# Linear-attention recurrence into a dropless MoE: the first six steps of the recurrence issued from a written-out table instead of the loop

## The chip, the core and the metric

The kernel runs on one core of a Trainium2 chip. The core has five engines that each work through a queue of their own, in order: PE (matrix multiply), DVE (VectorE, elementwise work, scans and reductions), ACT (ScalarE, exponentials, logarithms and copies), POOL (GpSimd, small elementwise work and indirect DMAs) and SP (SyncE, which issues nearly all the loads). An instruction starts when the one before it on its engine is done and the semaphores it waits for are there. So the order in which the program hands pieces of work to an engine decides what waits behind what.

The metric is the device time of one execution in microseconds (us), the median over several runs. An execution takes a little longer than the span between its first and its last profiled instruction.

## What is computed

The input is `q`, `k`, `v`, `f_logit` of shape (4, 8, 768, 48): batch, heads, tokens, channels. The reference runs a gated recurrence over the tokens, and sends its output through a mixture of eight experts in which every token goes to one expert:

```python
f = 1.0 / (1.0 + np.exp(-f_logit))
for t in range(S):                                   # S = 768
    state = f[:, :, t, :, None] * state + einsum('bhd,bhe->bhde', k[:, :, t], v[:, :, t])
    y[:, :, t] = einsum('bhd,bhde->bhe', q[:, :, t], state)
x = y.transpose(0, 2, 1, 3).reshape(3072, 384)
logits = x @ w_gate                                  # (3072, 8)
expert_idx = argmax(logits)
gate_w = softmax(logits)[expert_idx]
out = gate_w * (relu(x @ w1[expert_idx]) @ w2[expert_idx])   # w1: 384x1024, w2: 1024x384
```

## The kernel before, in words

**Tiling.** The 768 tokens are cut into 6 chunks of 128. A *unit* is one chunk of two of the four batches; there are NU = 12 units, and units 0, 2, 4, ... and 1, 3, 5, ... are two independent chains of states. A unit's `q`, `k` and `f` tile is 128 partitions by 8 segments by 128 tokens. Inside a chunk the recurrence becomes matrix work: with the running sum of the logarithms of `1 + exp(-f)` along the tokens, `k` is multiplied by the exponential of the sum ("r", growth) and `q` by the exponential of minus the sum ("dec", decay), and then a masked product of `k` and `q` gives the weights within the chunk.

**The pieces of one unit**, with the function, its line in the profile, its engine and its tile:

- `steps` L476 and `log` L484: ACT, exponential and logarithm of `f` into `g`
- `total` L491: DVE, the scan along the tokens, `g` to `sum`; it reads two tensors in SBUF (`g` and `cap`)
- `growth` L505: ACT, `r`, a tile with one buffer; `decay` L520: ACT, written over `g`
- `by_r` L509: `k <- k * r`, on POOL (on DVE for unit 0); it reads two tensors in SBUF
- `by_decay` L532: `q <- q * dec`, on DVE; it reads two tensors in SBUF
- `ends` L515 and `last_decay` L527: POOL, copies of 128x8
- `score` L543: PE, `s`, 16 products of `k` and `q`, in two halves a = 0, 1
- `mask` L549: DVE, four copies under a mask from PSUM into `at`; one input lies in SBUF
- `keys` L558: PE, transposes of `k`; `keep` L563: ACT, copies of them into `kn`
- `within` L571: PE, `yt` from `at` and `v`, in two halves; `before` L592: PE, the part of `yt` from the old state
- `added` L608: PE, `dp` from `kn` and `v`; `update` L623/L625: DVE, the new `state`, and then L627: POOL, `state` times `last`
- `settle` L633: ACT, `yt` to `ys`; `rows` L663: PE, transposed rows and gate logits `xp`, with a small DVE reduction L671 each half; `lay` L693/L688: ACT, rows into `xr`
- for every second unit the routing: `choose` (DVE, six small instructions, L214 to L222), `weigh` (ACT), `count` (PE, L226/L227), `place` and `fill` (DVE, nine small instructions, L233 to L260), `send` (POOL, indirect DMAs into `xs`).

`warm` L708 puts products of a zero tile on PE that nobody uses.

**What sets the order.** The block stands under `manual_schedule` for all five engines: each engine runs its instructions in the order in which the Python code calls them. Before the change the prologue issues units 0 to 2 piecewise by hand. Then one loop, `for n in range(1, NU + 2)`, issues for every step the scores, keys and masks of unit n, the halves of `within` of unit n - 1, the rows of unit n - 2, `by_r`, `ends`, `decay`, `last_decay` and `by_decay` of unit n + 1, `total` and `growth` of unit n + 2, `steps` of unit n + 3 and the loads of units n + 2 to n + 5. A dozen `if n == 1`, `if n == 2` and `1 < n < 4` in it shift pieces in the first steps.

One detail of `by_r` matters for the change. If the list `routed` holds an instruction, `by_r` takes it out and makes its POOL instruction wait for it:

```python
        def by_r(u, part=whole, on=nc.gpsimd):
            k = units[u]["k"][:, part]
            ins = on.tensor_tensor(k, k, units[u]["r"][:, part], op=OP.mult).ins
            if routed:
                tc.add_manual_dep(ins, routed.pop().name, SYNC, reason="the port of both")
```

The loop appends to `routed` the last instruction of `choose` (L222) or of `fill` (L260), from step 3 on. On DVE these stand shortly before the masks of the step. After the recurrence (units done at about 128 us) come the eight experts, PE work with the weights w1 and w2 streamed in.

Of the kernel before, what the change touches and what calls it, by code (L numbers as in the profile page):

```python
# [1 line left out]

# [8 lines left out]
F32 = mybir.dt.float32  # L11
# [3 lines left out]
OP = mybir.AluOpType  # L15
# [110 lines left out]
def kernel(  # L126
# [280 lines left out]
    def load_pads(e):  # L407
# [10 lines left out]
        tc.declare_no_dep(ins, group="xs", reason="no row is written twice")  # L418
        tc.add_to_no_dep_group("xs", ins)

    with ExitStack() as st:
        ld = st.enter_context(tc.tile_pool(name="ld", bufs=1))
        wk = st.enter_context(tc.tile_pool(name="wk", bufs=2))
# [99 lines left out]

        def last_decay(u):
            x = units[u]
            x["last"] = wk.tile([128, SEG], F32, name="last", bufs=3)
            nc.gpsimd.tensor_copy(x["last"], x["dec"][:, :, C - 1])  # L527

        def by_decay(u, part=whole):
# [35 lines left out]
        def within(u, a):  # L565

            x = units[u]
            if a == 0:
                x["yt"] = yt
            for p, h, _ in heads():  # L570
                nc.tensor.matmul(  # L571
                    x["yt"][DP * (h ^ a) : DP * (h ^ a) + D, a, p],
                    lhsT=x["v"][:, a, 2 * p + h],
                    rhs=x["at"][:, a, h, p],
                    start=p == 0,
                    stop=x["old"] is None,
                    skip_group_check=True,
                )
# [38 lines left out]
        def update(u):  # L617

            x = units[u]
            new = wk.tile([128, SEG, D], F32, name="state", bufs=4)  # L620
            last = _bc(x["last"], 2, D)
            if x["old"] is None:
                nc.vector.tensor_copy(new, x["dp"])  # L623
            else:
                nc.vector.tensor_tensor(new, x["dp"], x["old"], op=OP.add)  # L625
            states[u % 2] = new
            return lambda: nc.gpsimd.tensor_tensor(new, new, last, op=OP.mult)  # L627

        def settle(u):
            x = units[u]  # L630
# [64 lines left out]
        st.enter_context(tc.manual_schedule(engines=ordered))  # L695

        nc.scalar.preload_act_table_set("natural_log_exp_and_others")
        load(0, "f", ab)
        load(0, "kq")
        load(1, "f")  # L700
        load_first_consts()
        load(1, "kq")
        for i in (1, 0):
            nc.gpsimd.memset(scores[i], 0.0)
        def warm(count):

            for _ in range(count):
                nc.tensor.matmul(yt[:, 0, 0], lhsT=pad[:, 0:C], rhs=pad[:, 0:C], start=True, stop=True)  # L708

        warm(24)  # L710
        for part in ab:
            steps(0, part)
            total(0, part)
        load(2, "f")
        load(0, "v")
        for part in ab:
            growth(0, part)
            by_r(0, part, nc.vector)
            decay(0, part)
            by_decay(0, part)  # L720
        ends(0)
        last_decay(0)
        for part in ab:
            steps(1, part)
        load(3, "f")
        load(2, "k")
        load(1, "v")
        load(2, "q")
        load(3, "q")

        def early_banks():

# [38 lines left out]
            del sends[: len(now)]  # L771


        score(0, 0)
        score(0, 1)
        keys(0)
        warm(12)
        for part in ab:
            total(1, part)
        for a in range(2):  # L780
            for h in range(2):
                mask(0, a, h)
        for part in ab:
            growth(1, part)
            by_r(1, part)
        for part in ab:
            decay(1, part)
            by_decay(1, part)
        ends(1)
        last_decay(1)  # L790
        steps(2)
        total(2)
        keep(0)
        steps(3, logs=False)
        growth(2)
        load_consts()
        load(3, "k")
        load(4, "f")
        load(2, "v")
        load(5, "f")  # L800
        load_gate()

        for n in range(1, NU + 2):
            here, back, last = n, n - 1, n - 2
            ahead = n + 1 < NU
            state = n < NU - 2
            rt = None
            if here < NU:
                units[here]["old"] = states[here % 2]
            if 2 <= last:  # L810
                settle(last)
            if later and later[0] < NU - 1:
                later[1].weigh()
            if here < NU:
                for a in range(2):
                    score(here, a)
            if ahead and n != 2:
                by_r(n + 1)
                ends(n + 1)
            if decayed:  # L820
                decayed()
                decayed = None
            if sends:
                scatter_some(n)
            if n == NU - 2:
                soon = [load_rows(first[e]) for e in range(EARLY)]
            if n == 1:
                units[0]["old"] = None
                added(0)
                update(0)()  # L830
            if ahead and not 1 < n < 4:
                decay(n + 1)
                last_decay(n + 1)
            if state:
                keys(here)
                keep(here)
            if n == 2:
                growth(n + 1)
                by_r(n + 1)
                ends(n + 1)  # L840
            if 1 < n < 4:
                decay(n + 1)
                last_decay(n + 1)
            if here < NU:
                for a in range(2):
                    for h in range(2):
                        mask(here, a, h)
            if n == 1:
                log(3)
                within(0, 0)  # L850
                within(0, 1)
                settle(0)
            if n + 3 < NU:
                steps(n + 3)
            if later and n >= NU - 1:
                settled(*later)
                later = None
                scatter_some(NU)
            if 2 < n < NU - 2:
                total(n + 2)  # L860
            if n == NU - 2:
                by_decay(n + 1)
            first_half = 1 < n < NU - 2
            if first_half:
                within(back, 0)
            if 0 <= last:
                rt = rows(last, later[1] if later else None)
                lay(last)
            if later and n == NU - 2:
                settled(*later)  # L870
                later = None
                scatter_some(NU)
            if ahead and n < NU - 2:
                by_decay(n + 1)
            if n == 2:
                total(n + 2)
            if rt:
                rt.choose()
                if n < NU - 2:
                    routed.append(rt.latest)  # L880
                if n >= NU - 1:
                    rt.weigh()
            if later:
                settled(*later)
                routed.append(later[1].latest)
                later = None
            for a in range(int(first_half), 2):
                if 0 < back < NU:
                    within(back, a)
            if n == 2:  # L890
                settle(1)
            if n + 2 < NU and n != 1:
                growth(n + 2)
            if n == NU + 1:
                widen(soon[0], weights[0], early_h, range(3, 7))
            if n == NU:
                turn_early(soon[0])
            if state:
                added(here)
                decayed = update(here)  # L900
            if n == 1:
                total(3)
            if back < NU:
                before(back)
            if rt:
                later = (n, rt)
                if n >= NU - 1:
                    rt.count(turns("rp", [128, 2, rt.n, E]))
                if n >= NU:
                    settled(*later)  # L910
                    later = None
            if n == NU:
                early_h = early_banks()
                widen(soon[0], weights[0], early_h, range(3))
            if n == NU + 1:
                widen(soon[0], weights[0], early_h, range(7, NF))
                turn(soon[1])
            if n == 1:
                load(n + 3, "q")
            if n + 3 < NU:  # L920
                load(n + 3, "k")
            if n + 2 < NU:
                load(n + 2, "v")
            if 1 < n and n + 3 < NU:
                load(n + 3, "q")
            if n + 5 < NU:
                load(n + 5, "f")
            if n == 1:
                load_first_pads()
            if n in (8, 10):  # L930
                load_first_weights((n - 8) // 2)
                load_second_weights((n - 8) // 2)
# [395 lines left out]
```

## Time and profile before

| | |
|---|---|
| median of 9 runs | 401.79 us (400.85 to 403.5) |
| the profiled execution | 401.01 us, of which the span is 399.2 us |
| granted TensorE clock over the span | 0.986 |
| busy over the span: PE / DVE / ACT / POOL | 382.9 / 169.5 / 103.2 / 116.7 us |
| the chain that ended last | PE 87%, DMA 5%, DVE 2%, issue 2%, all else 1% or less each |
| where the chain first stays on PE for long | from 41.90 us (`dp`, L608) |

A row of the timeline reads: start in us, duration in us, engine, line, operation, output and input tiles, shapes, count, and in brackets the idle time of the engine just before it with what ended that idle time. A row of the stages reads: from:to, length, then for PE, PEld (weight loads), DVE, ACT and POOL the busy us and the instruction count, then the granted PE clock, the DMA share and GB/s.

### The profile page before, as it was taken

To read this page: it belongs to the slowest core of one execution; us is meant where nothing else is said; L and a number is where in the kernel's file an instruction comes from. 1 tells how busy PE (TensorE), PEld (TensorE's weight loads), DVE (VectorE), ACT (ScalarE), POOL (GpSimd) and SP (SyncE) were. 2 spreads that over 40 slices of the span, in tenths; PEclk is the share of its full clock that TensorE was granted. 3 is DMA by queue.
4 is the path that set the end of the run, shared out by engine and by line. 5 is a ranking of instruction groups with operands and counts; after the bars stand their busy time and mean duration, and the time that the engine had idled before them with its cause. 6 is when DMAs were issued, how large, how long until landed. Compare 5 with 4: busy or idle time off the path is not lost.

```text
span 399.2 us, 7726 instructions
## 1 busy us (share of the span) xinstructions
PE 382.9 (96%) x3062; PEld 268.8 (67%) x3062; DVE 169.5 (42%) x365; ACT 103.2 (26%) x190; POOL 116.7 (29%) x118
## 2 busy tenths in 40 slices
PE   7899999999996999999999999999999999999993
PEld 7778898998984987777555555664556556555453
DVE  6899987989651352203112113113713113111260
ACT  6998877774431100000010000001000000000000
POOL 5378868788534220010100100100100100100012
PEclk9999999999996899999999999999999999999999
DMA  8999667779677156959239899989146339995151
GB/s 277 377 369 366 200 221 260 239 213 339 208 212 296 41 158 210 316 140 307 85 135 350 232 372 398 272 340 347 39 148 215 84 125 396 395 418 182 15 185 42
DMA packets 51516, 95.05 MB, mean 238 GB/s; under 512 B 20824, under 2 KB 40731, under 8 KB 49424
## 3 DMA queue, kind: packets, MB, share of 16 engines
q1 hardware_dynamic: 48016, 84.76, 63.4%
q0 software_dynamic: 3168, 9.64, 6.4%
q8 instruction: 25, 0.41, 0.4%
q10 hardware_dynamic: 288, 0.08, 0.2%
q14 instruction: 19, 0.16, 0.1%
HBM read 79.46 MB, written 15.21 MB: 237 GB/s over the span
## 4 chain that ended last, share of the span: by engine, by line
PE 87%; DMA 5%; DVE 2%; issue 2%; SPq 1%; ACT 1%; POOL 0%; POOLq 0%; DVEq 0%; ACTq 0%
PE hps L316 27%; PE yps L332 23%; PE yps L1107 7%; PE xp L663 5%; PE yt L571 4%; PE s L543 4%; PE yt L592 4%; PE s L316 3%; PE hps L1081 3%; PE yp L332 3%; DMA fpack<-c_fpack 2%; DMA f<-in_fu_dram 2%; PE dp L608 2%; PE kp L558 2%; DMA fpack<-in_moe_w_gate_dram 1%
## 5 line engine op out<-in xcount | busy, mean ns | idle before, releaser
L316 PE MATMUL hps<-xT,w1t 128*128 128x352 f32 (+2 forms) x384 | 110.1, 447 | 0.0
L316 PEld LDWEIGHTS hps<-xT,w1t 128*128 128x128 f32 x384 | 72.7, 190 | 37.2 <-issue 1.9
L332 PE MATMUL yps<-w2t,hT 128*128 128x384 f32 x288 | 94.4, 487 | 0.0
L189 POOL DMA_INDIRECT out_dram<-ysb,dst x24 | 23.4, 974 | 224.4 <-DVE ysb L343 216.3
L332 PEld LDWEIGHTS yps<-w2t,hT 128*128 128x128 f32 x288 | 54.6, 190 | 38.6 <-issue 1.5
L326 ACT ACTIVATE hT<-hps 128x352 f32<-128x352 f32 (+2 forms) x28 | 13.8, 491 | 200.7 <-PE hps L316 190.6
L328 DVE TENSOR_SCALAR hT<-hps 128x352 f32<-128x352 f32 (+2 forms) x28 | 15.6, 558 | 93.0 <-PE hps L316 93.0
L343 DVE TENSOR_SCALAR ysb<-yps,tg 128x384 f32<-128x384 f32 x22 | 13.6, 617 | 74.4 <-PE yps L332 55.7
L189 POOL DMA_INDIRECT xs<-xr,posi x24 | 33.2, 1385 | 26.3 <-DVE counts L234 9.0
L549 DVE COPY_PREDICATED at<-mpack,s 128x512 f32<-128x512 uint8 x48 | 31.1, 728 | 6.2 <-PE s L543 6.2
L509 POOL TENSOR_TENSOR k<-k,r 128x1024 f32<-128x1024 f32 (+1 forms) x12 | 26.5, 2215 | 19.8 <-ACT r L505 10.4
L491 DVE TENSOR_TENSOR_SCAN sum<-g,cap 128x1032 f32<-128x1032 f32 (+1 forms) x14 | 28.8, 2059 | 3.2 <-ACT g L484 3.2
L543 PE MATMUL s<-q,k 64*128 64x128 f32 x384 | 24.9, 279 | 2.3 <-POOL last L527 1.6
L1107 PE MATMUL yps<-qw,hqT 128*32 128x192 f32 (+1 forms) x192 | 26.8, 380 | 0.0
L663 PE MATMUL xp<-fpack,ys 128*128 128x104 f32 x192 | 25.2, 281 | 0.5 <-DMA fpack<-in_moe_w_gate_dram 0.3
L543 PEld LDWEIGHTS s<-q,k 64*128 64x128 f32 x384 | 22.5, 188 | 4.5 <-POOL last L527 1.7
L571 PE MATMUL yt<-at,v 128*48 128x128 f32 x384 | 25.1, 277 | 0.0
L663 PEld LDWEIGHTS xp<-fpack,ys 128*128 128x128 f32 x192 | 22.8, 193 | 2.4 <-issue 1.8
L571 PEld LDWEIGHTS yt<-at,v 128*48 128x48 f32 x384 | 20.0, 123 | 2.6 <-issue 1.5
L1107 PE MATMUL yps<-w2t,hT 128*32 128x384 f32 x192 | 21.4, 487 | 0.0
L592 PE MATMUL yt<-q,state 48*48 48x128 f32 x320 | 15.4, 285 | 3.9 <-issue 3.9
L633 ACT COPY ys<-yt 128x512 f32<-128x512 f32 x24 | 12.9, 591 | 20.4 <-PE yt L592 20.4
(114 smaller groups left out, 367.0 us busy)
## 6 DMA issues: line engine op xcount, KB each, us to landing
qw<-in_moe_w_dram SPq DMA_DIRECT2D x16, 1536.0 KB
w1t<-in_moe_w_dram SPq DMA_DIRECT2D x8, 1536.0 KB
w2t<-in_moe_w_dram SPq DMA_DIRECT2D x8, 1536.0 KB
k<-in_ku_dram SPq DMA_DIRECT2D x12, 512.0 KB
q<-in_qu_dram SPq DMA_DIRECT2D x12, 512.0 KB
f<-in_fu_dram SPq DMA_DIRECT2D x11, 512.0 KB
xs<-pad SPq DMA_DIRECT2D x8, 600.0 KB
v<-in_vu_dram SPq DMA_DIRECT2D x12, 384.0 KB
```

The costliest lines, as they stand in the source:

```text
L189: ins = nc.gpsimd.indirect_dma_start(out=dst, out_offset=bass.IndirectOffsetOnAxis(ap=idx, axis=0), in_=src, in_offset=None, bounds_check= ...
L316: nc.tensor.matmul(x["h"][:, f], lhsT=w[0][:, j, b * 128 : b * 128 + 128], rhs=x["xT"][:, j], start=j == 0, stop=j == KD - 1,)
L328: nc.vector.tensor_scalar(to, x["h"], 0.0, None, op0=OP.max)
L332: nc.tensor.matmul(yp, lhsT=x["hT"][:, f, t * C : t * C + C], rhs=w[1][:, f, :], start=f == 0, stop=f == NF - 1,)
L491: nc.vector.tensor_tensor_scan(x["sum"][:, part].rearrange("p s c -> p (s c)"), x["g"][:, part].rearrange("p s c -> p (s c)"), cap[:, part ...
L509: ins = on.tensor_tensor(k, k, units[u]["r"][:, part], op=OP.mult).ins
L543: nc.tensor.matmul(ps[h][:, p], lhsT=x["k"][r, s], rhs=x["q"][r, s], start=True, stop=True)
L549: nc.vector.copy_predicated(x["at"][:, a, h], _bc(causal, 1, HP), x["ps", a][h])
L571: nc.tensor.matmul(x["yt"][DP * (h ^ a) : DP * (h ^ a) + D, a, p], lhsT=x["v"][:, a, 2 * p + h], rhs=x["at"][:, a, h, p], start=p == 0, st ...
L592: nc.tensor.matmul(x["yt"][to : to + D, a, p], lhsT=x["old"][r, HP * a + p], rhs=x["q"][r, HP * a + p], start=False, stop=True, skip_group ...
L663: nc.tensor.matmul(xp[:, p], lhsT=x["ys"][:, a, p], rhs=wx[:, p, 0:XW] if a else wx[:, p, E:WX], start=True, stop=True,)
L1107: nc.tensor.matmul(yp[r], lhsT=h[:, f, at : at + T], rhs=w[:, f, cols], start=f == 0, stop=f == NF - 1, skip_group_check=True,)
```

## The change

The prologue after the first memsets and the steps n = 1 to 5 of the loop are replaced by a table, `FIRST_STEPS`. Each word is a piece of work, a unit number and a half or phase: `scan4` is `total(4)`, `byr5` is `by_r(5)`, `mask2a` the two masks of unit 2's first half, `upd3` the DVE part of `update(3)` and `upd3p` its POOL part, `lf6` the load of `f` of unit 6, `fill17` is `warm(17)`. The words are issued in the order in which they stand; since every engine keeps its own queue, only the order among words of one engine counts. The loop then runs from n = 6, without its special cases. `routed` gets its first instruction after the table. The tile `last` has 4 buffers instead of 3; `within` sets `x["yt"]` for either half; the broadcast of `last` in `update` is made when it is used.

```diff
+    FIRST_STEPS = """
+        lf0a lk0 lq0 lf1 consts0 lk1 lq1 fill17 exp0a ln0a exp0b lf2 lv0 scan0a ln0b scan0b
+        dec0a r0a dec0b r0b byr0a byd0a exp1a ln1a exp1b lf3 lk2 lv1 lq2 lq3 last0 sc0a
+        byr0b byd0b scan1a ln1b dec1a sc0b kp0 fill6 r1a scan1b byd1a keep0 byr1a mask0a
+        mask0b ends0 dec1b r1b dp0 exp2 upd0 ln2 sc1a exp3 consts1 lk3 lf4 lv2 lf5 gate0 ln3
+        byr1b byd1b kp1 wi0b ends1 wi0a scan2 keep1 r2 set0 scan3 sc1b dp1 lq4 lk4 lv3 dec3
+        mask1a upd1 byr2 dec2 ends2 r3 mask1b byd2 byd3 wi1a ends3 kp2 last1 wi1b last2 exp4
+        lf6 pads0 sc2b ln4 keep2 mask2b sc2a lk5 lv4 lq5 byr3 upd0p mask2a exp5 lf7 xp0 lay0
+        sc3b set1 dp2 scan4 wi2b ln5 last3 upd2 r4 byr4 dec4 wi2a kp3 upd1p keep3 scan5 byd4
+        sc3a mask3b ends5 xp1 bef2 mask3a exp6 lk6 lv5 lq6 lf8 oh1 lay1 dp3 dec5 upd3 sc4a
+        mask4a set2 ln6 last5 upd2p sc4b kp4 r5 byd5 wi3b ends4 keep4 scan6 wi3a last4 xp2
+        wgh1 exp7 bef3 lk7 lv6 lq7 lf9 lay2 dp4 mask4b place1 ln7 upd4 scan7 byr5 ends6 sc5b
+        dec6 sc5a set3 r6 upd3p kp5 byd6 mask5a wi4a wi4b keep5 exp8 xp3 byr6 bef4 lk8 lv7
+        lq8 lf10 ln8 lay3 dp5 r7 set4 mask5b oh3 upd4p last6 upd5 wgh3 send5
+    """
...
-            x["last"] = wk.tile([128, SEG], F32, name="last", bufs=3)
+            x["last"] = wk.tile([128, SEG], F32, name="last", bufs=4)
...
-        warm(24)
-        for part in ab:
-            steps(0, part)
-            total(0, part)
...
-        score(0, 0)
-        score(0, 1)
-        keys(0)
-        warm(12)
...
-        for n in range(1, NU + 2):
+        FIRST = 6
+        routes, waiting = {}, {}
...
+        DO = {
+            "exp": lambda u, p: steps(u, piece(p), logs=False),
+            "ln": lambda u, p: log(u, piece(p)),
+            "scan": lambda u, p: total(u, piece(p)),
+            "r": lambda u, p: growth(u, piece(p)),
+            "byr": lambda u, p: by_r(u, piece(p), nc.gpsimd if u else nc.vector),
...
+            "upd": lambda u, p: waiting.pop(u)() if p else do_update(u),
...
+        for what, u, part in re.findall(r"([a-z]+)(\d+)([abp]?)", FIRST_STEPS):
+            DO[what](int(u), part)
+        routed.append(routes[FIRST - 3].latest)
+        later, decayed = (FIRST - 1, routes[FIRST - 3]), waiting.pop(FIRST - 1)
+
+        for n in range(FIRST, NU + 2):
...
-            if ahead and n != 2:
+            if ahead:
                 by_r(n + 1)
                 ends(n + 1)
```

More of the change, by code (lines that the diff above doesn't have):

```diff
@@ L1 @@
+import re
 from contextlib import ExitStack
@@ L567, in within @@
             x = units[u]
-            if a == 0:
-                x["yt"] = yt
+            x["yt"] = yt
             for p, h, _ in heads():
@@ L620, in update @@
             new = wk.tile([128, SEG, D], F32, name="state", bufs=4)
-            last = _bc(x["last"], 2, D)
             if x["old"] is None:
@@ L626, in update @@
             states[u % 2] = new
-            return lambda: nc.gpsimd.tensor_tensor(new, new, last, op=OP.mult)
+            return lambda: nc.gpsimd.tensor_tensor(
+                new, new, _bc(x["last"], 2, D), op=OP.mult
+            )
         def settle(u):
@@ L697 @@
         nc.scalar.preload_act_table_set("natural_log_exp_and_others")
[L698 to L702, printed above, removed]
         for i in (1, 0):
@@ L708, in warm @@
                 nc.tensor.matmul(yt[:, 0, 0], lhsT=pad[:, 0:C], rhs=pad[:, 0:C], start=True, stop=True)
-        warm(24)
-        for part in ab:
-            steps(0, part)
-            total(0, part)
[L714 to L729, printed above, removed]
         def early_banks():
@@ L771, in scatter_some @@
             del sends[: len(now)]
-        score(0, 0)
-        score(0, 1)
-        keys(0)
-        warm(12)
[L778 to L801, printed above, removed]
-        for n in range(1, NU + 2):
+        FIRST = 6
+        routes, waiting = {}, {}
+        def old_of(u):
+            if "old" not in units[u]:
+                units[u]["old"] = states[u % 2] if u > 1 else None
+        def do_added(u):
+            old_of(u)
+            added(u)
+        def do_update(u):
+            waiting[u] = update(u)
@@ new lines, in do_within, with do_rows, do_place, piece @@
+        def do_within(u, part):
+            old_of(u)
+            within(u, "ab".index(part))
+        def do_rows(u):
+            routes[u] = rows(u, routes.get(u - 1))
+            if routes[u] is None:
+                del routes[u]
+        def do_place(u):
+            settled(u + 3, routes[u])
+        def piece(part):
+            return ab["ab".index(part)] if part else whole
+        DO = {
[4 more added lines that the diff above has]
+            "byr": lambda u, p: by_r(u, piece(p), nc.gpsimd if u else nc.vector),
+            "ends": lambda u, p: ends(u),
+            "dec": lambda u, p: decay(u, piece(p)),
+            "last": lambda u, p: last_decay(u),
+            "byd": lambda u, p: by_decay(u, piece(p)),
+            "sc": lambda u, p: score(u, "ab".index(p)),
+            "mask": lambda u, p: [mask(u, "ab".index(p), h) for h in range(2)],
+            "kp": lambda u, p: keys(u),
+            "keep": lambda u, p: keep(u),
+            "wi": do_within,
+            "bef": lambda u, p: before(u),
+            "dp": lambda u, p: do_added(u),
+            "upd": lambda u, p: waiting.pop(u)() if p else do_update(u),
+            "set": lambda u, p: settle(u),
+            "xp": lambda u, p: do_rows(u),
+            "lay": lambda u, p: lay(u),
+            "oh": lambda u, p: routes[u].choose(),
+            "wgh": lambda u, p: routes[u].weigh(),
+            "place": lambda u, p: do_place(u),
+            "send": lambda u, p: scatter_some(u),
+            "fill": lambda u, p: warm(u),
+            "lf": lambda u, p: load(u, "f", ab if p else (whole,)),
+            "lk": lambda u, p: load(u, "k"),
+            "lq": lambda u, p: load(u, "q"),
+            "lv": lambda u, p: load(u, "v"),
+            "consts": lambda u, p: (load_first_consts, load_consts)[u](),
+            "gate": lambda u, p: load_gate(),
+            "pads": lambda u, p: load_first_pads(),
+        }
@@ L806 @@
             state = n < NU - 2
-            rt = None
             if here < NU:
                 units[here]["old"] = states[here % 2]
-            if 2 <= last:
+            if n > FIRST:
                 settle(last)
-            if later and later[0] < NU - 1:
+            if n > FIRST and later and later[0] < NU - 1:
                 later[1].weigh()
@@ L826 @@
                 soon = [load_rows(first[e]) for e in range(EARLY)]
[L827 to L831, printed above, removed]
+            if ahead:
                 decay(n + 1)
@@ L836 @@
                 keep(here)
[L837 to L843, printed above, removed]
             if here < NU:
@@ L847 @@
                         mask(here, a, h)
[L848 to L852, printed above, removed]
             if n + 3 < NU:
@@ L858 @@
                 scatter_some(NU)
-            if 2 < n < NU - 2:
+            if n < NU - 2:
                 total(n + 2)
@@ L862 @@
                 by_decay(n + 1)
-            first_half = 1 < n < NU - 2
+            first_half = n < NU - 2
             if first_half:
                 within(back, 0)
-            if 0 <= last:
-                rt = rows(last, later[1] if later else None)
-                lay(last)
+            rt = rows(last, later[1] if later else None)
+            lay(last)
             if later and n == NU - 2:
@@ L874 @@
                 by_decay(n + 1)
-            if n == 2:
-                total(n + 2)
             if rt:
@@ L889 @@
                     within(back, a)
-            if n == 2:
-                settle(1)
-            if n + 2 < NU and n != 1:
+            if n + 2 < NU:
                 growth(n + 2)
@@ L900 @@
                 decayed = update(here)
-            if n == 1:
-                total(3)
             if back < NU:
@@ L917 @@
                 turn(soon[1])
-            if n == 1:
-                load(n + 3, "q")
             if n + 3 < NU:
@@ L923 @@
                 load(n + 2, "v")
-            if 1 < n and n + 3 < NU:
+            if n + 3 < NU:
                 load(n + 3, "q")
@@ L927 @@
                 load(n + 5, "f")
-            if n == 1:
-                load_first_pads()
             if n in (8, 10):
```

## The prediction, made before the changed kernel ran

> **What bounds the kernel now.** I read the page first. The change ends where step 5 ends, so only the left sixth of the slices can move.
>
> ```profile
> PE   7899999999996999999999999999999999999993
> ...
> DVE  6899987989651352203112113113713113111260
> ACT  6998877774431100000010000001000000000000
> POOL 5378868788534220010100100100100100100012
> PEclk9999999999996899999999999999999999999999
> ```
>
> A slice is 10 us. DVE is at 8 or 9 tenths from 10 to 60 us, PE at 8 or 9, so I looked at stages of 10 us:
>
> ```profile
> 10.00:20.00 10.00, 8.37 (x121) 7.78 (x118) 8.96 (x11) 9.00 (x17) 3.63 (x4) 1.00 1.00 376
> 20.00:30.00 10.00, 9.07 (x145) 8.00 (x142) 9.80 (x13) 9.29 (x14) 7.43 (x6) 1.00 1.02 370
> 30.00:40.00 10.00, 9.18 (x132) 8.30 (x132) 9.13 (x11) 8.64 (x15) 8.96 (x7) 1.00 1.01 365
> 40.00:50.00 10.00, 9.46 (x158) 8.39 (x156) 9.36 (x17) 8.32 (x15) 8.72 (x8) 1.00 0.64 200
> 50.00:60.00 10.00, 10.00 (x169) 9.08 (x169) 8.69 (x21) 7.72 (x14) 6.27 (x6) 1.00 0.62 219
> ```
>
> Up to about 42 us PE is not full and DVE is (9.80 of 10). From there PE is full: the chain of waits stays on PE from 41.90, and PE has no idle row from 41.90 until 114 us. So the time is the moment at which the unbroken PE stretch can begin, and DVE sets that. What a faster start can win is bounded by PE's useless time before 41.90: the second fillers (12.79, 2.84 us) and the idle rows 1.59, 0.57, 0.28, 0.82 and 0.54 us, together 6.6 us. DVE's and POOL's rows in the timeline show what DVE loses:
>
> ```profile
> 29.83 2.37 POOL L509 TENSOR_TENSOR k<-k,r 128x1024 f32<-128x1024 f32 x1 [1.14 <-ACT r L505]
> ...
> 31.56 1.72 DVE L532 TENSOR_TENSOR q<-q,g 128x1024 f32<-128x1024 f32 x1
> ...
> 32.13 1.20 POOL L515 COPY rend<-sum 128x8 f32<-128x8 f32 x1
> ...
> 33.20 2.30 DVE L491 TENSOR_TENSOR_SCAN sum<-g,cap 128x1032 f32<-128x1032 f32 x1
> ...
> 33.27 2.21 POOL L527 COPY last<-g 128x8 f32<-128x8 f32 x1
> ...
> 36.73 2.37 POOL L509 TENSOR_TENSOR k<-k,r 128x1024 f32<-128x1024 f32 x1 [1.03 <-ACT r L505]
> ...
> 38.35 2.91 DVE L491 TENSOR_TENSOR_SCAN sum<-g,cap 128x1032 f32<-128x1032 f32 x1
> ...
> 39.04 2.20 POOL L515 COPY rend<-sum 128x8 f32<-128x8 f32 x1
> ```
>
> Read them as one lock that DVE's two-SBUF-input instructions (scan, q, k) and POOL's instructions hold in turn, each to its end. The scan at 38.35 takes 2.91 us instead of 2.30: POOL's k multiply ends at about 39.05, and 39.05 + 2.21 (the scan's start-to-start time at 47.68) is its end, 41.26. The q at 31.56 takes 1.72 instead of 1.22 (50.64) for the same reason. The other way round, the 128x8 copies of POOL take 2.20 instead of 0.20 behind a scan. And where POOL already waits, it gets in *between two DVE instructions that stand directly behind each other*: the copy at 32.13 ends at 33.33, right at the end of q (33.28), though the scan was queued. The masks (one SBUF input) and the state copies don't take part:
>
> ```profile
> 44.45 2.38 POOL L509 TENSOR_TENSOR k<-k,r 128x1024 f32<-128x1024 f32 x1 [1.28 <-DVE ex L222]
> ...
> 53.74 2.38 POOL L509 TENSOR_TENSOR k<-k,r 128x1024 f32<-128x1024 f32 x1 [3.57 <-DVE xr L260]
> ```
>
> These two, held back by the "port of both" wait, run beside the masks (45.19 and 54.56, 2.60 us each, undisturbed), and the scans behind those take 2.29 and 2.30.
>
> **The change part by part.** The built program's order by engine shows: SP issues the same loads in the same order. DVE does the same instructions up to the state update of unit 5 (62.17 in the trace), in another order. So I make a ledger of DVE from the first mask (13.87) to that update: the work cancels, only its waits count.
>
> *Waits that go.* Port: q 23.36 (1.53 - 1.22), scan 25.29 (2.62 - 2.30), q 31.56 (0.50), scan 38.35 (0.61), q 41.36 (1.75 - 1.22): 2.3 us. Inputs, by the idle column: 0.27, 0.20, 0.17, 0.70, 0.51, 0.48, 0.60, 0.28: 3.2 us. I grant that nearly all of these go, since DVE becomes the late one; 0.4 us stays (0 to 1.5).
>
> *Waits that come.* In the table no k multiply has the "port of both" wait, and it stands so that POOL is free before its r is ready. By unit, with start-to-start times from the rows (POOL k 2.31, scan 2.21, q 1.13, mask 0.62, state 0.45; ACT 0.96 for 1024 columns, settle 0.95, lay 0.8):
> - Unit 2: POOL waits behind two scans and starts with the masks of unit 1. No loss.
> - Unit 3: DVE's queue is two masks, state, two masks (2.95 us), q2, q3. The tile r has one buffer, so r3 starts when the k2 multiply ends, 2.31 after the scan, and is ready at 3.3, while q2 runs (2.95 to 4.08). POOL waits, gets the port at 4.08, and q3 waits 2.31.
> - Unit 4: DVE is at scan4, state, scan5, q4. ACT reaches r4 0.5 after scan4 (lay 0.8, settle 0.95, ln 0.96 from the reductions on, less 2.21) and ends it at 1.46, inside scan5 (0.45 to 2.66). POOL gets the port at its end: q4 waits 2.31.
> - Unit 6: r6 is ready 4.6 after the reductions (lay, ln, dec, settle, r); DVE has masks 1.24, the nine small ones 1.65, state 0.45, so scan7 runs from 3.3 to 5.55. q6 waits 2.31.
> - Unit 5: r5 is ready 4.6 after the reductions, q5 is reached at 4.0 to 4.8. POOL first: q5 waits; q5 first: scan6 behind it waits. 1.7 to 2.3, I take 2.0.
> - Unit 1: r1a is ready within 0.15 us of the end of scan1b, so POOL may come first or not: 0 to 1.4 (the half multiply), I take 0.7.
> - Small: after the k4 multiply POOL's backlog of copies and two state products (0.83 at 24.91) falls among the six small instructions of `choose`: 0 to 1.0, I take 0.8.
>
> Together 3 x 2.31 + 2.0 + 0.7 + 0.8 = 10.4 us come. Sum: 10.4 + 0.4 - 2.3 - 3.2 = **+5.3 us** on DVE at unit 5's update. PE can't win it back, since it is full from there on with the same work, and needs the masks and q of DVE. Against the profiled execution (401.0, span 399.2 and 1.8 around it): 406.3. The median before stands 0.8 above that execution, so I say **407.1**. The bounds of these terms give +3.1 to +7.7; if one of the three certain collisions is missed, +0.8. Own range 402.6 to 409.5.
>
> *The rest costs nothing.* A fourth buffer of `last` (128x8) and the later broadcast add no instruction. The score halves split on PE lie beside DVE's work; if DVE were not late, they could cost the 0.5 us between two masks that they wait for. Fillers go from 24 + 12 to 17 + 6: PE waits for q at 9.5 anyway; the cover is gone only if the clock drops (below). The loads and their issue (0.33 us and more each) stay where they were in SP's queue.
>
> *The skill.* The Trainium skill, "SBUF — State Buffer", "Who interferes with whom", says that the order of issue decides who blocks, for the whole instruction; the rows above agree. The same page, "A bandwidth-pool intuition that's wrong", speaks against me: it has GpSimd resume some 115 ns after the end of the DVE instruction, and by that a queued DVE instruction would be first at each boundary. By that sentence units 3, 4 and 6 would lose nothing and the sum would be that of rival A; the row at 32.13 (in by 0.05 us after q) is why I don't take it.
>
> **The rivals.**
> - *A, faster: DVE wins the boundary.* The POOL row that slips in is a copy of 128x8; no row shows a 2.31 us multiply wait behind a DVE instruction with another queued. If the long one does not get in, it runs later beside the masks, where the table has it (`byd3 ... byr3 ... mask2a`). Units 1, 3, 4 and 6 then cost nothing and unit 5 about 1.0: 1.0 + 0.8 + 0.4 - 2.3 - 3.2 = -3.3 on DVE; but 0.51 + 0.48 + 0.60 + 0.28 of the waits counted were for a PE already full, so -1.4 is left: 400.4, with 398.5 and 401.8 as ends. It decides at the first boundary, scan1b or q2.
> - *B, no change.* Loads hold the start: the DMA share is 1.0 from 10 to 40 us. Against it: DVE waited 0.3 us for a load, ACT 0.4 (after the 0.95 at 10.03), PE 0.3. With the load order unchanged, or if the table is in effect the loop's order, 401.8.
> - *C, slower still: the clock.* With 13 fillers (3.1 us) fewer, the granted clock may fall early, as in 120:130, where it was 0.60 at 6.61 us busy. 5.5 us of real PE work between 10 and 20 would take 3.7 more, and idle time there hides about half: +2 on the forecast, 409.1.
>
> **How the numbers follow.** Forecast 0.66, A 0.18, B 0.08, C 0.08. A measurement here tells about 0.3% (1.2 us) from no change. Faster holds most of A and a little of B, 0.14; within 0.3% the rest of A and B and the forecast's low end, 0.13; slower 0.73. The range reaches into A to 400.2 and up to 409.6; left out are A's better half and the tail beyond C.
>
> **What would show it.** In the changed profile's timeline: a q row (L549) of about 3.4 us (2.31 + 1.13) directly behind q2, scan5 and scan7, each beside a k row of POOL (L526) that itself took longer than 2.37 because it waited; DVE idle for inputs near 0 from 14 to 60 us; idle rows of PE of 1 to 3 us before `dp` of units 3 to 6; the update of unit 5 at about 67.5. q rows near 1.2 and k rows of 3 us or more beside masks would prove A; a PEclk under 9 in the first slices, C. If the boundaries go DVE's way I am wrong in sign.

## The result, and the profile after

| | before | after |
|---|---|---|
| median | 401.3 us (53 runs) | 402.94 us (16 runs, 400.48 to 404.38) |
| span of the profiled execution | 399.2 us | 400.4 us |
| granted TensorE clock over the span | 0.986 | 0.983 |

The ratio after to before is 1.0033, with an interval of 1.0021 to 1.0046: slower by 0.8 to 1.8 us, about 1.3. (The two medians of the table differ by 1.64 us; what follows goes by the ratio and its interval.) The forecast was +5.3 us. The sign is that of the forecast and POOL's multiplies push in between DVE's instructions as it said; the size is a quarter of it, and one step of its reasoning failed.

The slices of the page of the kernel after, for the engines that matter here:

```profile
PE   7989898999995999999999999999999999999993
...
DVE  6999999889660352213112113113713113111260
...
PEclk9999999999996899999999999999999999999998
```

DVE is at 9 tenths from 10 to 70 us; PE drops to 8 in three slices there. The clock row is that of before up to the last slice, so in this case the fewer fillers cost no clock. The stages of the same kernel (same columns as before: from:to, length, PE, PEld, DVE, ACT, POOL, clock, DMA share, GB/s):

```profile
20.00:30.00 10.00, 8.32 (x127) 7.15 (x126) 10.00 (x9) 9.43 (x15) 7.70 (x7) 1.00 0.91 332
30.00:40.00 10.00, 9.18 (x129) 8.21 (x128) 9.84 (x10) 6.95 (x14) 4.57 (x6) 1.00 0.98 362
40.00:50.00 10.00, 8.69 (x151) 7.89 (x151) 9.86 (x18) 6.87 (x13) 6.09 (x9) 1.00 0.72 251
50.00:60.00 10.00, 9.09 (x155) 8.21 (x155) 9.79 (x17) 7.71 (x13) 3.90 (x4) 1.00 0.56 193
60.00:70.00 10.00, 8.82 (x145) 7.93 (x144) 9.62 (x19) 7.20 (x14) 8.82 (x9) 1.00 0.73 234
```

Before, PE was full from 42 us on (10.00 in the stage 50:60). Now it is short of full by 0.9 to 1.3 us in every stage from 40 to 70 us, and DVE has hardly a gap. Where DVE's time goes is in the timeline of after, the rows of DVE and POOL (L508 is now the scan, L549 `q`, L526 the k multiply):

```profile
24.98 4.53 DVE L549 TENSOR_TENSOR q<-q,g 128x1024 f32<-128x1024 f32 x2
25.48 2.95 POOL L526 TENSOR_TENSOR k<-k,r 128x1024 f32<-128x1024 f32 x1 [0.64 <-ACT r L522]
...
35.97 3.48 POOL L526 TENSOR_TENSOR k<-k,r 128x1024 f32<-128x1024 f32 x1 [5.43 <-ACT r L522]
37.21 3.33 DVE L549 TENSOR_TENSOR q<-q,g 128x1024 f32<-128x1024 f32 x1
...
46.71 3.27 POOL L526 TENSOR_TENSOR k<-k,r 128x1024 f32<-128x1024 f32 x1 [1.35 <-ACT r L522]
47.68 4.47 DVE L508 TENSOR_TENSOR_SCAN sum<-g,cap 128x1032 f32<-128x1032 f32 x1
...
57.08 2.93 POOL L526 TENSOR_TENSOR k<-k,r 128x1024 f32<-128x1024 f32 x1 [3.89 <-ACT r L522]
57.77 3.32 DVE L549 TENSOR_TENSOR q<-q,g 128x1024 f32<-128x1024 f32 x1
```

For comparison, `q` of unit 5 in the kernel before, without a collision:

```profile
50.64 1.22 DVE L532 TENSOR_TENSOR q<-q,g 128x1024 f32<-128x1024 f32 x1
```

The pairs of rows of after are the collisions of units 3, 4, 5 and 6. Take the second: POOL's multiply is issued at 35.97, while the scan of DVE runs until 37.2. Its row is 3.48 us long and not 2.37, because it waited. At the scan's end it gets the port (the lock that the prediction read out of the rows), although `q` stands queued on DVE, and `q` takes 3.33 us for 1.22. The four cost DVE 2.2, 2.11, 2.17 and 2.10 us. A fifth, small one is in `choose` (44.09, 0.82 us for 0.19). At unit 1 there was none. PE then waits before `dp`, in PE's rows of the same timeline:

```profile
42.42 1.14 PE L624 MATMUL dp<-v,kn 128*64 128x48 f32 x32 [1.31 <-ACT xr L710]
...
52.79 1.14 PE L624 MATMUL dp<-v,kn 128*64 128x48 f32 x32 [0.91 <-ACT xr L710]
...
62.99 1.14 PE L624 MATMUL dp<-v,kn 128*64 128x48 f32 x32 [1.18 <-ACT xr L710]
```

The way there is: `q` late, so the masks and the reductions `lg` behind it on DVE late, so ACT's copies into `xr` late, which `dp` on PE waits for. The chain of waits of after (start, us, piece) runs over the same collisions, where that of before was on PE from 41.90. (Between the first two rows shown it goes over POOL's copies and a load of `v`, 6.38 us from 30.84.)

```profile
25.48 2.95 POOL k L526
...
37.22 3.32 DVE q L549
...
47.76 4.39 DVE sum L508
...
57.86 3.24 DVE q L549
```

From 62.99 on PE runs without a gap until 116 us. What is left of DVE's lateness is told by rows of PE and DVE, here those of before:

```profile
60.26 1.09 PE L608 MATMUL dp<-v,kn 128*64 128x48 f32 x32
61.28 1.44 PE L592 MATMUL yt<-q,state 48*48 48x128 f32 x32
62.65 2.06 PE L543 MATMUL s<-q,k 64*128 64x128 f32 x32
...
62.17 0.56 DVE L625 TENSOR_TENSOR state<-dp,state 128x384 f32<-128x384 f32 x1 [0.28 <-PE dp L608]
63.84 2.60 DVE L549 COPY_PREDICATED at<-mpack,s 128x512 f32<-128x512 uint8 x4 [1.11 <-PE s L543]
```

And those of after (`dp`, at 62.99, is shown above; L608 is now `before`):

```profile
60.72 1.09 PE L608 MATMUL yt<-q,state 48*48 48x128 f32 x32
...
64.06 2.06 PE L560 MATMUL s<-q,k 64*128 64x128 f32 x32
...
65.10 0.56 DVE L640 TENSOR_TENSOR state<-dp,state 128x384 f32<-128x384 f32 x1 [0.25 <-PE dp L624]
65.57 2.60 DVE L566 COPY_PREDICATED at<-mpack,s 128x512 f32<-128x512 uint8 x4
```

The state update of unit 5 on DVE starts at 65.10 and not 62.17: +2.93. PE's scores of unit 6 start at 64.06 and not 62.65: +1.41. And +1.4 it stays to the scores of the last unit (108.57 for 107.17), with the span +1.2. These are differences of one trace each. Two kernels below (units 5, and 5 to 7 delayed) are the kernel before up to unit 5, and have their scores of unit 5 at 53.64 and 53.81 where before has 53.37, so some 0.4 us of such a difference can be scatter.

### The profile page after: what moved, and what is told of

Read it like the earlier page. It is cut to its first block, busy times and chain, and to the rows that moved or that the text cites. A ratio compares the mean times of both kernels' runs of the same rounds, so it can differ in the third digit from the quotient of the medians.

```text
span 400.4 us, 7645 instructions
## 1 busy us (share of the span) xinstructions
PE 381.1 (95%) x3036; PEld 267.5 (67%) x3036; DVE 175.7 (44%) x365; ACT 101.9 (25%) x190; POOL 108.2 (27%) x118
## 4 chain that ended last, share of the span: by engine, by line
PE 82%; DVE 6%; ACT 4%; DMA 3%; issue 2%; POOL 1%; SPq 0%; POOLq 0%; ACTq 0%
PE hps L317 27%; PE yps L333 23%; PE yps L1109 7%; PE xp L680 4%; PE yt L587 3%; PE s L317 3%; PE s L560 3%; PE hps L1083 3%; PE yp L333 3%; PE yt L608 2%; DVE q L549 2%; DMA f<-in_fu_dram 2%; DVE sum L508 2%; DMA v<-in_vu_dram 2%; DVE at L566 2%
## 5 line engine op out<-in xcount | busy, mean ns | idle before, releaser
L317 PEld LDWEIGHTS hps<-xT,w1t 128*128 128x128 f32 x384 | 72.7, 190 | 37.2 <-issue 1.9
L190 POOL DMA_INDIRECT xs<-xr,posi x24 | 30.5, 1272 | 26.0 <-DVE su L260 10.3
L526 POOL TENSOR_TENSOR k<-k,r 128x1024 f32<-128x1024 f32 (+1 forms) x12 | 30.1, 2510 | 25.1 <-ACT r L522 20.5
L508 DVE TENSOR_TENSOR_SCAN sum<-g,cap 128x1032 f32<-128x1032 f32 (+1 forms) x14 | 30.1, 2159 | 3.0 <-ACT g L501 2.9
L549 DVE TENSOR_TENSOR q<-q,g 128x1024 f32<-128x1024 f32 (+1 forms) x14 | 21.2, 1520 | 0.0
```

The lines of the kernel that those rows point to most:

```text
L190: ins = nc.gpsimd.indirect_dma_start(out=dst, out_offset=bass.IndirectOffsetOnAxis(ap=idx, axis=0), in_=src, in_offset=None, bounds_check= ...
L317: nc.tensor.matmul(x["h"][:, f], lhsT=w[0][:, j, b * 128 : b * 128 + 128], rhs=x["xT"][:, j], start=j == 0, stop=j == KD - 1,)
L508: nc.vector.tensor_tensor_scan(x["sum"][:, part].rearrange("p s c -> p (s c)"), x["g"][:, part].rearrange("p s c -> p (s c)"), cap[:, part ...
L549: nc.vector.tensor_tensor(q, q, x["dec"][:, part], op=OP.mult)
```

## The experiments

The theory after this comparison: the table in itself is faster, the port takes the gain away, and PE pays for only a part of what DVE loses. The rival: the table's order on PE and ACT is what costs, and the port waits are hidden.

### All four collisions taken away, then three, then one

In the table kernel the k multiply of a unit waits until DVE is through with the instruction it collided with. For units 3, 4 and 6 that is `q`, for unit 5 the scan behind `q`; the word `byr4` goes behind `byd4`. Nothing is computed otherwise.

```diff
+        HOLD = {3: ("byd", 3), 4: ("byd", 4), 5: ("scan", 6), 6: ("byd", 6)}
...
+            if u in HOLD:
+                tc.add_manual_dep(ins, made[HOLD[u]].name, SYNC, reason="the port of both")
...
-        ... r4 byr4 dec4 wi2a kp3 upd1p keep3 scan5 byd4 ...
+        ... r4 dec4 wi2a kp3 upd1p keep3 scan5 byd4 byr4 ...
```

> The table as changed, but POOL's k multiplies of units 3, 4 and 6 wait for the q multiply of the same unit and that of unit 5 for the scan of unit 6, so that they start beside the masks (the word byr4 moves behind byd4 for it). Theory 1, the port: the four collisions (2.1 to 2.2 us of DVE each in the changed kernel's trace) go, no q or scan row is above 2.5 us, and the scores of unit 6 start 3 to 5 us earlier than 64.06, at 59 to 61; time 1.5 to 3.5 us under the kernel before, ratio 0.991 to 0.996. Theory 2, the order on PE and ACT (dp of a unit waits for the copies of the rows, which wait for reductions that the table puts behind a q and two masks): the collisions lie beside that wait, and the time stays within 1 us of the changed kernel, ratio 1.001 to 1.005.

Measured: 398.4 us, ratio to before 0.9936 (0.9916 to 0.9957). The same without the wait of unit 5:

> As the run with all four waits, but unit 5's k multiply stays free and meets the scan of unit 6. Theory 1: between the changed kernel and the run with four waits, 0.5 to 2 us above the latter, with one scan row of about 4.4 us at 45 to 50. Theory 2: as the changed kernel, ratio 1.001 to 1.005.

Measured: 399.55 us, 0.9962 (0.9942 to 0.9981). And with the wait of unit 3 alone, and `byr4` where the table had it:

> The changed kernel with the wait for unit 3's k multiply alone. Theory 1: a single collision is worth what DVE loses less the slack behind it, 0.7 to 2.1 us, so the time is 0.997 to 1.002 of the kernel before. Theory 2: no difference to the changed kernel that can be told, ratio 1.002 to 1.005.

Measured: 400.76 us, 0.9985 (0.9963 to 1.0007).

The theory holds and the rival falls: with every DVE and PE word of the table where it was, and POOL's multiplies held back, the table is 0.6% faster than before, not 0.3% slower. PE's scores of unit 6 start at 59.69 with all four waits, 60.00 without that of unit 5, 62.86 with that of unit 3 alone, 64.06 with none. So unit 3's wait is worth 1.2 us on PE, those of 4 and 6 together 2.9. With unit 5's collision left in (a scan of 4.48 us at 44.86) PE lost 0.6 us of its 2.2: from the scores of unit 4 to those of unit 5 it is 9.97 us for 9.39, and 0.3 us are left at unit 6 because this trace was 0.27 ahead at unit 4. The medians differ by 1.15 us, in intervals that overlap. Most of this one collision is absorbed. Whether that is the place of unit 5 or that it stood alone, no run separates.

### A loss seen in that run, mended

In the run with all four waits PE had one idle row left after 31 us. Its timeline shows POOL's two indirect sends and then the multiply of unit 7, and what PE waits for:

```profile
59.73 1.17 POOL L190 DMA_INDIRECT xs<-xr,posi  x1 [0.17 <-DMA v<-in_vu_dram]
61.21 0.97 POOL L190 DMA_INDIRECT xs<-xr,posi  x1 [0.30 <-issue]
62.18 2.40 POOL L528 TENSOR_TENSOR k<-k,r 128x1024 f32<-128x1024 f32 x1
...
68.31 1.14 PE L628 MATMUL dp<-v,kn 128*64 128x48 f32 x32 [1.11 <-ACT xr L714]
```

The multiply stands behind the sends until 62.18, runs into DVE's scan of 64.42 (3.24 us for 2.30), and of the 3.0 us won at unit 6's scores 1.6 are lost before unit 7's (1.3 at the last unit's). POOL had been idle from 51 to 56 us. So:

```diff
-        r6 upd3p kp5 ... wgh3 send5
+        r6 upd3p send5 kp5 ... wgh3
```

> The table with the four waits, and the word for the two indirect sends moved in the table from behind unit 6's multiply on POOL to ahead of it (POOL stood idle there from 51.0 to 56.27 us). Port theory: with the waits alone the two sends (59.73 and 61.21) held unit 7's multiply until 62.18, and 1.3 us of the 3.0 us that had been won at unit 6's scores were lost again before unit 7's. With the sends early, unit 7's multiply starts at about 60.5, its scan is no longer lengthened from 2.30 to 3.24, the PE idle row of 1.11 at 68.31 goes: about 397.4 us, ratio 0.989 to 0.992. Rival (PE is full and only its own sum counts): 398.4 as before, ratio 0.9936.

Measured: 397.7 us, ratio to before 0.99 (0.9865 to 0.9935). The multiply of unit 7 starts at 60.67 and the idle row is gone; the scan, expected to be free, is still lengthened, to 2.83 at 63.31. The interval of the ratio overlaps that of the run without the move, so the 0.7 us between the medians aren't settled by the times; PE's own rows show it more sharply (scores of unit 7 at 69.26 for 70.68, of the last unit at 104.11 for 105.48). This is the fastest version found. Its stages, to be held against those of after:

```profile
30.00:40.00 10.00, 10.00 (x161) 9.21 (x162) 9.38 (x13) 7.46 (x15) 3.92 (x7) 1.00 0.97 367
40.00:50.00 10.00, 10.00 (x181) 9.00 (x174) 8.88 (x17) 7.96 (x17) 4.38 (x9) 1.00 0.74 249
50.00:60.00 10.00, 10.00 (x184) 9.13 (x182) 9.61 (x23) 8.53 (x15) 7.28 (x8) 1.00 0.74 245
```

PE is full from 31 us on, 11 us earlier than before the change. Held against it, after's scores start later by 2.21 us at unit 4, 3.18 at unit 5, 4.44 at unit 6 and 4.49 at unit 7: that is what four collisions, 8.6 us of DVE, cost PE (at unit 7 the moved sends have a part in it). DVE's own update of unit 5 is only 4.75 us later (65.10 for 60.35). Without the collisions DVE waits for inputs more (1.94 us for 0.41 from the first masks to that update), and three other rows are lengthened beside POOL, by 1.6 us in all (2.96 for 2.30 at 31.43, 0.87 for 0.24 at 50.38, 0.47 for 0.19 at 59.19).

### The wait that the loop had, taken away from the kernel before

```diff
-            if routed:
+            if False:
```

> The kernel before, its loop's order untouched, without the wait called the port of both: in every step from n = 4 on POOL's k multiply starts as soon as its r and PE let it. Theory 1: it meets the q or the scan in most steps (rows of 3.3 or 4.5 us); DVE has about 1 us of slack for each step there, so about 1 us stays for each of the six or so steps, 3 to 7 us slower, ratio 1.007 to 1.017. Theory 2, a DVE that is late does not set the end: ratio 0.998 to 1.003.

Measured: 404.26 us, 1.0076 (1.0048 to 1.0104). So the loop's "port of both" wait is worth about 3 us. But the rows that were expected to grow did not: from 50 us on `q` and scan take 1.21 and 2.29. What pays is a small instruction of the routing, in the timeline of this kernel:

```profile
53.84 2.38 POOL L509 TENSOR_TENSOR k<-k,r 128x1024 f32<-128x1024 f32 x1 [5.43 <-ACT r L505]
54.03 0.19 DVE L251 TENSOR_REDUCE posi<-place 128x4 int32<-128x32 f32 x1
54.14 0.17 DVE L258 TENSOR_REDUCE su<-ex 128x4 f32<-128x32 f32 x1
54.35 1.90 DVE L259 TENSOR_SCALAR su<-su 128x4 f32<-128x4 f32 x1
```

POOL's multiply comes in between two small ones; the two reductions run beside it undisturbed, and the next, an instruction of 128x4 that took 0.17 us before, lasts until the multiply's end. It happens in each of seven steps: three times to this instruction (1.73 us lost each), and four times, in the steps with `choose`, to a product or comparison of 128x32 that took 0.19 (2.08 to 2.18 us lost each). That makes 13.8 us of DVE. The run lost 3 us, PE 4.1 us at the last unit's scores. The idle time before the masks, 6.2 us in the whole run of before, is 0.0 in this one. That slack can have taken up to 6.2 us of the loss.

### A delay of DVE without any port

The step of the forecast that "DVE late is PE late" can be tried by itself. Two reductions over a constant tile, 2.27 us in all, stand ahead of the masks of some units of the kernel before. Nobody reads their result. The diff is that for unit 5; the others have other units in its first line.

```diff
+            if here in (5,):
+                for i in range(2):
+                    nc.vector.tensor_reduce(spare[:, i : i + 1], cap.rearrange("p s c -> p (s c)"), axis=AX_X, op=OP.max)
             if here < NU:
```

In unit 5 alone:

> The kernel before, with the two reductions in unit 5 alone: 2.2 us of DVE. The prediction's step: 2.2 less the 0.60 that DVE waited for the scores = +1.6 us, about 402.8, PE's scores of unit 6 at 64.2. Theory of absorbed delays: +0.4 us or nothing, 401.2 to 401.6, scores of unit 6 at about 63.

Measured: 401.88 us, 1.0018 (0.9997 to 1.0038). The times can't tell the two; the trace can. Rows of DVE and PE in the timeline of this kernel:

```profile
54.14 2.35 DVE L847 TENSOR_REDUCE spare<-cap 128x1 f32<-128x1032 f32 x2
56.41 2.57 DVE L549 COPY_PREDICATED at<-mpack,s 128x512 f32<-128x512 uint8 x4
...
61.82 1.14 PE L608 MATMUL dp<-v,kn 128*64 128x48 f32 x32 [1.12 <-ACT xr L693]
62.89 1.09 PE L592 MATMUL yt<-q,state 48*48 48x128 f32 x32
63.91 2.06 PE L543 MATMUL s<-q,k 64*128 64x128 f32 x32
```

The masks had waited 0.60 us for the scores; that wait is gone, and 1.67 us of delay are left. `dp` waits 1.12. From the scores of unit 5 to those of unit 6 it is 10.27 us (63.91 - 53.64), before 9.28 (62.65 - 53.37): PE loses 0.99. The prediction's step said 1.6 and absorption 0.4; the truth lies between. After that the steps have their old lengths. The rows tell where the rest of the 1.67 went. Before, ACT's copy into `xr` ended at 59.95 (59.47 and 0.48) and PE reached `dp` only at 60.26: 0.31 of slack. The two reductions `lg` had waited about 0.12 between them. And `before`, behind `dp`, took 1.37 us to the scores and takes 1.02 here: 0.35. Together that is 0.78, for 0.68 to be explained.

In units 5, 6 and 7:

> The kernel before, with the same two reductions in each of units 5, 6 and 7, where PE runs without a gap: 6.6 us of DVE. The prediction's step (PE is full and needs the masks, so it can't win anything back; less DVE's waits for the scores, 0.60 + 1.11 + about 1): +3.9 us, about 405.1. Theory of absorbed delays (without the old wait for the port each step lost 1.8 to 2.2 us on DVE in its small instructions, some eight times, and the run only 2.7 to 3.1 us): +1 us, about 402.2.

Measured: 404.38 us, 1.0062 (1.0035 to 1.0088), so +2.5 us, and in PE's scores +0.99, +0.44, +1.17 for the three, nothing in the fourth and -0.32 in the fifth step: +2.28. Again between the two. In units 2, 3 and 4:

> The kernel before, with two reductions over a constant tile ahead of the masks in each of units 2, 3 and 4: about 1.1 us each, 2.2 us of DVE a unit, 6.6 in all, as long as three waits for the port, but with no port and no consumer. The prediction's step (DVE late is PE late, less the waits of DVE in the trace, 0.17 + 0.70 + 0.51): +5.2 us, about 406.4. Theory of absorbed delays (the four waits of the table cost 4.5 us at the end for 9.2 us of DVE): +3.2 us, about 404.4, PE's scores of unit 6 at about 65 for 62.65.

Measured: 406.13 us, 1.0109 (1.0065 to 1.0154), so +4.4 us (2.6 to 6.2), from four runs; against before, PE's steps are longer by 0.92, 2.50 and 0.76. The interval holds both expectations, and these steps can't be read as the delay alone. First, the 0.92 of unit 2 is in other kernels too: in the three other kernels that are the kernel before up to there, the step from the scores of unit 2 to those of unit 3 takes 9.96, 10.23 and 10.29 us, here 10.19, and 9.27 in before. So no cost of the delay in unit 2 shows. Second, the granted clock fell in this run, as the page's clock row (fifth slice) and PE's rows show:

```profile
PEclk9999899999997799999999999999999999999997
```

```profile
43.99 1.14 PE L608 MATMUL dp<-v,kn 128*64 128x48 f32 x32 [2.19 <-ACT xr L693]
45.06 1.93 PE L592 MATMUL yt<-q,state 48*48 48x128 f32 x32
46.92 2.81 PE L543 MATMUL s<-q,k 64*128 64x128 f32 x32
49.67 1.09 PE L558 MATMUL kp<-fpack,k 128*128 128x128 f32 x8
```

From 45 to 48 us the clock was 0.57, 0.50 and 0.50. `before` took 1.86 us to the next start for 1.02, the scores 2.75 for 1.99: 0.84 and 0.76, together 1.6 us that are clock. What remains is 1.66 in unit 3 and nothing in unit 4. The 1.66 is the whole delay less what it removed: behind the reductions the scan of 41.05 takes 2.30 us, where before it took 2.91 beside POOL. The times agree: three of the four executions had a mean clock of 0.974 to 0.978 (before: 0.982 to 0.99); the fourth, at 0.986, took 403.6 us, 2.2 above before.

Together: of 2.27 us of DVE, PE pays 0.4 to 1.2 us where it is full. In the early units it pays nothing that shows in unit 2 and 1.66 in unit 3, where DVE's masks had not waited for PE and PE already waited 0.54 us for `xr`; unit 4 says nothing, since PE itself was late there. Neither full transfer nor full absorption describes it.

## Why the prediction was right in sign and wrong in size

- **The port goes to the one that waits: right.** Units 3, 4 and 6 lose at `q` as worked out; in unit 5 `q` came first and the scan behind it waited, one of the two cases named. Rival A (DVE wins at the boundary) is refuted by the four pairs of rows above, and with it what the prediction inferred from the Trainium skill, "SBUF — State Buffer" ("A bandwidth-pool intuition that's wrong"). The page gives DVE's end plus some 115 ns for a DMA whose descriptors GpSimd writes; that a queued DVE instruction would be first is not in it, and here a multiply of 2.3 us got in between two DVE instructions that stood directly behind each other.
- **The sum of the collisions: a little too large.** Less the old port waits, 8.1 us were forecast (10.4 - 2.3). The rows of `q`, scan and `ex` grew by 5.04 + 1.16 + 0.65 = 6.85. Unit 1 cost 0 and not 0.7, each collision 2.1 to 2.2 and not 2.31: by its end the multiply had begun a little before `q` could have (39.45 less 2.37 is 37.08, for a start of `q` at 37.21).
- **Input waits: right.** DVE's idle time in the stretch went from 3.21 to 0.41 us; 3.2 and 0.4 were said.
- **Not in the ledger:** the rest of the stretch became 0.65 us shorter, which I can't lay to single rows, and the stretch began 0.47 earlier (13.40 for 13.87), the load of `f` of unit 1 being early (ACT starts on it at 9.56 for 10.03). That is scatter: in three other kernels with the table's prologue the same `q` starts at 12.85, 13.28 and 13.76. So DVE's update came 2.93 late and not 5.3; these 2.37 us, the collisions' 1.25 among them, are the larger part of the miss.
- **The step that failed: "PE can't win it back, since it is full from there on with the same work, and needs the masks and q of DVE."** Being full says that PE wasn't waiting, not that DVE was just in time. The forecast passed DVE's lateness on whole; of 2.93 us only 1.41 arrived, and with no port in play PE paid 0.44 to 1.17 of 2.27 where it was full. Before, DVE stood ahead of PE: its masks waited 0.51, 0.60 and 1.11 us for the scores in units 4 to 6. The last of these lies behind the point to which I took the ledger, the update of unit 5, and so was not in the sum. After, the masks of unit 6 follow the update at once (65.57). And "the same work" left out its order: the loop has `before` of unit 4 between `dp` of unit 5 and the scores of unit 6 (61.28), the table has it ahead of `dp` (60.72), where PE would have waited anyway. `dp` is 2.73 us late, but the scores follow it after 1.07 us and not 2.39. Those 1.32, and 0.20 between `dp` and the update, are the 1.52. The two are one thing seen from either engine: the masks' 1.11 us were a wait for scores that stood behind `before`. No run has the one order of PE with the other's DVE, so how much the order alone saves is not shown.
- **The terms together:** 5.3 - 1.25 (collisions) - 0.65 - 0.47 - 1.52 (not passed on to PE) = 1.41 us, which is PE's difference in the traces, with the scatter named above; the times say 0.8 to 1.8. The waits of PE before `dp` were forecast at 1 to 3 us for units 3 to 6; they are 1.31, 0.91 and 1.18 for units 3 to 5, and none for unit 6.
- **The table alone: a gain**, as the bound of 6.6 us had left room for. With the four waits it is 2.6 us faster than before (1.7 to 3.4), with the two sends moved as well 4.0 (2.6 to 5.4). Rivals B and C are out: the ratio's interval leaves out 1, and with the order of the loads untouched the time falls when POOL's multiplies are held back; and the clock row did not fall.

What stays open: units 6 and 7 of the delayed kernel were not taken apart as unit 5 was, and each reading rests on one trace. Nor is it settled how much of the 0.7 us of the moved sends is real in the time.

## What to carry to other kernels

An order written by hand must carry over the waits that an old order had for a shared port: here the table with such waits was 0.6% faster than before (1.0% with two sends moved as well), and without them 0.3% slower, because four multiplies of POOL were issued just before DVE's two-input instructions. When a delay on one engine is to be priced on another that looks full, carry the ledger to the instruction of the *full* engine and subtract the waits that the delayed engine has for it, the last one too, and the time by which its results lie ready. Look also at what the full engine can do while it waits, if the new order offers it other work there. Where a POOL multiply must run beside DVE, give it a wait that starts it with DVE's masks or reductions.

## What the runs showed of the hardware

- A POOL multiply of 2.3 us that waits behind a DVE instruction gets the port at its end even if another DVE instruction is queued; in the kernel after it happened in all four cases (`q` to `q` at 24.98, scan to `q` at 37.21 and 57.77, `q` to scan at 47.68).
- A small DVE instruction waits as a large one does: one of 128x4 (0.17 us) took 1.90 us beside a multiply, though it reads a single tensor. Reductions of 128x32 from SBUF (0.19 and 0.17 us at 54.03 and 54.14), and long ones over 128x1032 (2.27 us for two), did not wait; nor did the masks.
- Of seven collisions with small instructions, 13.8 us on DVE, 3 us came through to the time; the idle time before the masks, 6.2 us over the run, went to 0.0.
- After a pause of PE of 2.19 us (before the row at 43.99) the granted clock fell to 0.50 to 0.57 from 45 to 48 us, in the kernel with units 2 to 4 delayed. PE's pauses of 1.31, 0.91 and 1.18 us in the kernel after were followed by no such fall. Whether the pause is the cause, one trace doesn't show.
